# Pooled sums of q and k for the first two batches by accumulated TensorE products, with a new order of steps

## The chip, the cores and the metric

The kernel runs on one core of a Trainium2 chip. A core has a matrix engine (TensorE, PE in the profile), a vector engine (VectorE, DVE), an activation engine (ScalarE, ACT), a general engine (GpSimd, POOL) and a queue from which all transfers of this kernel start (SyncE, SP). Products land in PSUM, which has eight banks; all else lies in SBUF. Each engine works through its own queue in the order in which the program wrote it, and waits for the others by semaphores. The metric is device time in microseconds (us); lower is better.

## What is computed

The inputs are q, k and v of 8 batches, 8 heads, 576 tokens and 64 channels in float32, and the weights of a feed-forward layer, which arrive as float64 (512 x 1024 and 1024 x 512, with a scale vector). Cut to what matters:

```python
q_d = q.reshape(B, H, 144, 4, D).mean(axis=3)      # likewise k_d, v_d
out_up = np.repeat(sm_attn(q_d, k_d, v_d), 4, axis=2)
mask = np.abs(pos[:, None] - pos[None, :]) < 4
out_local = softmax(scale * q @ k.T where mask) @ v
x = (out_up + out_local) as [4608 tokens, 512]
h = x @ w_in
solu = h * softmax(h)
ln = (solu - mean) / np.sqrt(var + 1e-06) * g_ln
out = ln @ w_out
```

The attention has a pooled part, in which four neighbouring tokens are added up to one of 144 (the division by four is put into later scales), and a local part, in which a token sees three neighbours on each side.

## The kernel before

**Attention, batch by batch.** The 8 heads are taken as 4 pairs. For each pair, q and k are turned so that channels lie on partitions (`qT`, `kT`, 128 x 576: 64 channels of two heads), and then summed over four tokens (`qd`, `kd`, 128 x 144). `Batch.pair_steps` does that with VectorE transposes and two `sums` (line 419, a VectorE reduction). The first two batches are `EarlyBatch`: q and k are loaded so that a partition holds six neighbouring tokens (96 partitions, `TT` = 6), and `EarlyBatch.pair_steps` turns them with TensorE: for each of six token phases t and two heads, a product of the data with the unit matrix (line 557, tiles `qp` and `kp`), into a tile of two PSUM banks of which 288 numbers each are used. A copy (lines 263 on ScalarE or 265 on VectorE) brings them to `qT` and `kT` in token order, and the two `sums` follow as steps 5 and 6 of the pair.

`Pooled` makes the scores of 144 by 144 tokens (line 788, `sd`), the softmax (lines 795 to 812), turns it (line 823, `pdt`) and multiplies by the pooled v (line 844, `po`). `Local` and, from batch 3, `PairOfLocals` do the local part in windows of 64 tokens: scores (lines 607 and 695, `sc`), softmax, turning (line 655, `plt`), product with v (lines 665 and 753, `xp`).

**The feed-forward part** takes 36 tiles of 128 tokens. `xhl` splits x into two numbers `xh` and `xl` of reduced width (lines 1017 and 1020), `ffn_in` makes h with 24 products of 512 columns (line 862), and the softmax, the mean and the variance; `ffn_back` and `ffn_ut` turn the result by way of device memory and VectorE; `ffn_out` makes the output with 24 products (line 986). The weights are brought from float64 to pairs of reduced numbers in 16 pieces (`Weights.piece`, lines 364 to 412).

**Fillers.** `keep_clock` issues two products of no use (line 1043, tile `warm`); 24 such steps are in the plan.

**The order.** The functions above are generators. A plan lists all their steps in a natural order: 24 fillers first, then batch by batch the loads, pairs, attention, weights and feed-forward tiles. `ORDER` is a permutation of the plan's numbers, and the steps are run, that is written to the engines' queues, in that order; nothing is reordered afterwards. A step whose number is in `OTHER` uses a second engine for its work where the code offers one (`engine(usual, instead)`). Since the two early batches have 6 steps for each pair, the plan has 2029 steps.

```python
    for n in ORDER.split():
        now[0] = int(n)
        fn, args = plan[now[0]]
        fn(*args)
```

Of the kernel before, what the change touches and what calls it, by code (L numbers as in the profile page):

```python
# [137 lines left out]
def pooled_local_attention_then_solu_ffn(  # L138
# [10 lines left out]
    nc = tc.nc  # L149
# [884 lines left out]
    def row(steps, n):  # L1034
        for _ in range(n):
            step(next, steps)
# [119 lines left out]
```

## Time and profile before

| | |
|---|---|
| median of 3 runs | 589.33 us (589.28 to 589.5) |
| the profiled execution | 585.0 us |
| its span, first to last instruction | 583.2 us |
| mean granted TensorE clock | 0.999 |
| busy: PE, DVE, ACT, POOL | 564.1, 469.3, 333.8, 299.5 us |
| moved by DMA | 99.59 MB |

The profile is of one execution. A row of a group gives the line, the engine, the operation, the tile written and those read, the shapes, the count, the busy time in us and the mean of one instruction in ns, and behind the second bar the idle time of the engine ahead of it. A row of a timeline begins with the start in us from the span's start and the length. A row of waits names the engine and line that waited, the one that it waited for, and the us in total, the number of times and the longest. In the rows by stage, each engine has its busy us in the stage and its number of instructions. The ends of matmul records are modelled, so a step's length is read from its start to the start of the next one; a float32 product takes two records.

### The profile page before, as it was taken

The page shows a single profiled execution, that of the slowest core. Times are in us where ns is not written, and L with a number is a line of the kernel's source. Part 1 is how long each engine was busy: PE and PEld are TensorE (multiplying, and loading weights), DVE is VectorE, ACT ScalarE, POOL GpSimd, SP SyncE. Part 2 cuts the span into 40 slices and gives each one's busy share as a digit, 9 for nine tenths or more (in the row PEclk, how much of TensorE's full clock was granted, in tenths as well). Part 3 has the DMA queues.
Part 4 walks back from the last instruction along what each step waited for, and adds up shares of the span by engine and source line. Part 5 has one row for each costly group of instructions (what it writes and reads, how often), then busy time and mean ns, then how long its engine had stood idle before and what let it go on. Part 6 is the DMA issues. An engine that isn't in the chain of part 4 may idle for free.

```text
span 583.2 us, 15261 instructions
## 1 busy us (share of the span) xinstructions
PE 564.1 (97%) x5852; PEld 434.1 (74%) x5852; DVE 469.3 (80%) x779; ACT 333.8 (57%) x750; POOL 299.5 (51%) x447
## 2 busy tenths in 40 slices
PE   7899998999999999999999999999999999999996
PEld 3676666777787777877777777777787777788875
DVE  7989999898988879998977967899878877545541
ACT  4778678468546646565565753466445654444442
POOL 3657677957454745648533546356433752334120
PEclk9999999999999999999999999999999999999999
DMA  8997767787877888876867976766755145304230
GB/s 280 286 213 187 189 148 193 200 193 171 228 160 185 188 191 169 194 198 157 208 153 195 228 190 167 212 157 159 195 163 148 56 145 164 127 36 163 90 110 37
DMA packets 207113, 99.59 MB, mean 171 GB/s; under 512 B 163136, under 2 KB 193344, under 8 KB 207040
## 3 DMA queue, kind: packets, MB, share of 16 engines
q1 hardware_dynamic: 207040, 98.61, 66.3%
q8 instruction: 46, 0.75, 0.6%
q14 instruction: 27, 0.22, 0.1%
HBM read 65.54 MB, written 27.79 MB: 160 GB/s over the span
## 4 chain that ended last, share of the span: by engine, by line
PE 64%; DVE 14%; SPq 7%; DMA 5%; ACT 4%; issue 3%; POOL 2%; POOLq 0%; DVEq 0%
PE o L986 27%; PE h L862 25%; SPq L286 4%; DMA v<-u 3%; PE po L844 2%; PE sd L788 2%; PE xp L753 1%; PE pdt L823 1%; PE sc L607 1%; PE sc L695 1%; DVE w L375 1%; DVE qd_flat L419 1%; DVE nmx L870 1%; SPq L942 1%; DVE e L877 1%
## 5 line engine op out<-in xcount | busy, mean ns | idle before, releaser
L986 PE MATMUL o<-wo_h,uh 128*128 128x512 f32 x288 | 116.6, 405 | 1.5 <-ACT osb L993 0.8
L862 PE MATMUL h<-wi_h,xh 128*128 128x512 f32 x288 | 116.9, 406 | 0.8 <-DVE e L877 0.6
L862 PE MATMUL h<-wi_h,xl 128*128 128x512 f32 x288 | 114.1, 396 | 0.7 <-POOL xl L1020 0.7
L986 PE MATMUL o<-wo_l,uh 128*128 128x512 f32 x288 | 113.8, 395 | 0.0
L862 PE MATMUL h<-wi_l,xh 128*128 128x512 f32 x288 | 113.7, 395 | 0.0
L986 PE MATMUL o<-wo_h,ul 128*128 128x512 f32 x288 | 78.9, 395 | 0.0
L972 POOL TENSOR_TENSOR ul<-v,uh 128x512 fp32r<-128x512 f32 x40 | 51.9, 1297 | 42.8 <-ACT uh L969 41.6
L874 ACT ACTIVATE e<-h,nmx 128x1024 f32<-128x1024 f32 x36 | 40.2, 1116 | 49.1 <-DVE nmx L870 45.5
L986 PEld LDWEIGHTS o<-wo_h,uh 128*128 128x128 f32 x288 | 54.0, 188 | 16.8 <-ACT osb L993 1.5
L862 PEld LDWEIGHTS h<-wi_h,xh 128*128 128x128 f32 x288 | 54.1, 188 | 15.8 <-issue 2.9
L862 PEld LDWEIGHTS h<-wi_h,xl 128*128 128x128 f32 x288 | 54.1, 188 | 15.4 <-POOL xl L1020 2.1
L986 PEld LDWEIGHTS o<-wo_h,ul 128*128 128x128 f32 x288 | 54.0, 188 | 13.4 <-DVE ul L972 0.3
L870 DVE TENSOR_REDUCE nmx<-h 128x1 f32<-128x1024 f32 x36 | 43.8, 1216 | 24.2 <-PE h L862 24.2
L986 PEld LDWEIGHTS o<-wo_l,uh 128*128 128x128 f32 x288 | 54.1, 188 | 12.0
L862 PEld LDWEIGHTS h<-wi_l,xh 128*128 128x128 f32 x288 | 54.1, 188 | 11.9
L877 DVE SCALAR_TENSOR_TENSOR e<-h,e 128x1024 f32<-128x1024 f32 x36 | 43.8, 1217 | 14.2 <-ACT e L874 14.0
L969 ACT ACTIVATE uh<-v 128x512 fp32r<-128x512 f32 x70 | 42.9, 624 | 18.5 <-issue 7.1
L963 DVE STREAM_TRANSPOSE v<-v 128x512 f32<-128x512 f32 x70 | 46.4, 689 | 7.6 <-DMA v<-u 7.5
L993 ACT ACTIVATE osb<-o,s 128x512 f32<-128x512 f32 x36 | 24.6, 682 | 40.0 <-PE o L986 22.1
L1020 POOL TENSOR_TENSOR xl<-x,xh 128x512 fp32r<-128x512 f32 (+1 forms) x26 | 32.9, 1268 | 22.5 <-ACT xh L1017 22.2
L487 POOL TENSOR_TENSOR vs<-vs 72x512 f32<-72x512 f32 x24 | 31.9, 1328 | 17.5 <-DMA vs<-in_v_dram 9.0
L882 POOL TENSOR_SCALAR nmu<-su 128x1 f32<-128x1 f32 x36 | 8.1, 226 | 60.1 <-DVE e L877 57.2
(128 smaller groups left out, 1116.3 us busy)
## 6 DMA issues: line engine op xcount, KB each, us to landing
u<-e SPq DMA_DIRECT2D x35, 512.0 KB
v<-u SPq DMA_DIRECT2D x140, 128.0 KB
vs<-in_v_dram SPq DMA_DIRECT2D x32, 288.0 KB
out_dram<-osb SPq DMA_DIRECT2D x36, 256.0 KB
qm<-in_q_dram SPq DMA_DIRECT2D x96, 72.0 KB
km<-in_k_dram SPq DMA_DIRECT2D x96, 72.0 KB
vw<-in_v_dram SPq DMA_DIRECT2D x80, 64.0 KB
vw<-in_v_dram SPq DMA_DIRECT2D x40, 128.0 KB
```

What stands on the lines that cost most here:

```text
L286: nc.sync.dma_start(t[nm][Q * 32:Q * 32 + 32, pr], src[b, 2 * pr + par, :, dh * 32:dh * 32 + 32].rearrange("(k t) d -> t k d", t=32),)
L487: eng.tensor_tensor(out=vs[:, :, 0:2 * D], in0=vs[:, :, 0:2 * D], in1=vs[:, :, 2 * D:4 * D], op=ALU.add)
L862: nc.tensor.matmul(hps[:, n, :], src[:, cc, :], wt[:, cc, n * 512:(n + 1) * 512], start=(cc == 0 and src is xh and wt is wi_h), stop=(cc = ...
L870: nc.vector.tensor_reduce(out=nmx, in_=hf, op=ALU.max, axis=AX.X, negate=True)
L874: nc.scalar.activation(e, hf, AF.Exp, bias=nmx, scale=1.0, accum_out=se)
L877: nc.vector.scalar_tensor_tensor(out=e, in0=hf, scalar=1.0, in1=e, op0=ALU.mult, op1=ALU.mult, accum_out=su)
L963: nc.vector.transpose(vg, vg)
L969: nc.scalar.activation(uh, tp, AF.Copy)
L972: (usual if v is None else engine(usual, nc.vector)).tensor_tensor(out=ul, in0=tp, in1=uh.bitcast(F32), op=ALU.subtract)
L986: nc.tensor.matmul(o, src[:, j, :], wt[:, 4 * g + j, :], start=(g == 0 and j == 0 and src is uh and wt is wo_h), stop=(g == 1 and j == 3 a ...
L993: nc.scalar.activation(osb, o, AF.Copy, scale=s)
L1020: engine(nc.gpsimd, nc.vector).tensor_tensor(out=l, in0=src, in1=h.bitcast(F32), op=ALU.subtract)
```

## The change

For the batches below `POOLED_ON_PE` = 2, `pair_steps` adds, behind the twelve products that turn q or k, fourteen more in the same PSUM tile: the 144 numbers behind the 288 of its first bank. Token 6p + t belongs to the pooled token (6p + t) // 4, so with p = 2m + e the pooled token is 3m + (6e + t) // 4: for each phase t, the products take the columns of the unit matrix for e = 0 and 1 and add into columns j of every m, accumulating over t. For t = 2 the two columns don't lie at a step that one output can have, and two products of 48 columns are made. The copy step then also copies the 144 sums to `qd` or `kd` on the same engine, the two `sums` steps fall away, and the plan has 2013 steps. `ORDER` and `OTHER` are new as a whole. In the new order the first loads of q and k are issued ahead of the first weight piece, and three filler steps stand ahead of the first turning, where seven stood before.

```diff
 ORDER = """
-7 192 160 6 193 194 24 195 196 197 161 162 25 163 164 8 165 198 199 166 168 167 169 170 176 12
-171 172 177 33 22 1 3 32 26 178 15 27 28 29 30 31 41 20 173 179 174 34 180 35 181 36 37 40 64
...
+18 21 24 25 184 8 26 30 27 20 185 186 187 31 28 29 152 188 189 32 33 190 34 56 153 154 155 156
+191 35 3 66 160 161 67 37 68 157 158 159 36 38 39 43 162 163 164 165 40 166 167 57 42 192 193
...
 """
@@
     FIRST_ON_PE = ()
+    POOLED_ON_PE = 2
@@ class EarlyBatch
+        by_pe = property(lambda self: self.b < POOLED_ON_PE)
@@ EarlyBatch.pair_steps
                             ident[0:self.TP, 0:self.TP], start=True, stop=True,
                         )
+                if self.by_pe:
+                    three = tp[:, 0, n:n + SD].rearrange("x (m j) -> x m j", j=3)
+                    turn = ident[0:self.TP, 0:self.TP].rearrange("p (m e) -> p m e", e=2)
+                    for at_t, (t, js, es) in enumerate((
+                        (0, (0, 2, 1), (0, 2)), (1, (0, 2, 1), (0, 2)),
+                        (2, (2, 3, 1), (1, 2)), (2, (0, 1, 1), (0, 1)), (3, (0, 3, 2), (0, 2)),
+                        (4, (1, 3, 1), (0, 2)), (5, (1, 3, 1), (0, 2)),
+                    )):
+                        for par in range(2):
+                            nc.tensor.matmul(
+                                three[rows(par), :, js[0]:js[1]:js[2]],
+                                self.qk[nm, pr][:, par, t],
+                                turn[:, :, es[0]:es[1]], start=at_t == 0, stop=at_t == 6,
+                            )
                 yield
                 copy(
                     engine(nc.scalar, nc.vector),
                     dst.rearrange("x (p a t) -> x p a t", a=2, t=HT),
                     tp[:, :, 0:n].rearrange("x a (t p) -> x p a t", t=HT),
                 )
-                yield
+                if self.by_pe:
+                    copy(
+                        engine(nc.scalar, nc.vector),
+                        self.qd[pr] if nm == "q" else self.kd[:, pr], tp[:, 0, n:n + SD],
+                    )
+                yield
+            if self.by_pe:
+                return
             sums(self.qd[pr], self.qT[:, pr])
             yield
             sums(self.kd[:, pr], self.kT[:, pr])
@@ prepare
-            row(bt.pair_steps(pr), 6 if bt.b < EARLY else 4)
+            row(bt.pair_steps(pr), 6 if POOLED_ON_PE <= bt.b < EARLY else 4)
```

201 rows, old and new, of tables (ORDER, OTHER) are left out of this document.

## The prediction

> **What bounds the kernel now.** I read the page's first two parts, then the busy time by stage, then TensorE's own timeline and waits, and last the groups. First the page: totals, then TensorE (PE) and VectorE (DVE) in 40 slices.
>
> ```profile
> PE 564.1 (97%) x5852; PEld 434.1 (74%) x5852; DVE 469.3 (80%) x779; ACT 333.8 (57%) x750; POOL 299.5 (51%) x447
> ...
> PE   7899998999999999999999999999999999999996
> ...
> DVE  7989999898988879998977967899878877545541
> ```
>
> PE is busy throughout; DVE is as full only in the first fifth. What a change early in the kernel is worth is therefore read from that fifth, and what it leaves behind must still pass through PE. I cut the span where PE changes its work: the first turned q (9.75), the first product of the feed-forward part (57.30), the first product of token tile 4 (118.60), and the last product's end.
>
> ```profile
> core 0: us, PE busy (x) PEld busy (x) DVE busy (x) ACT busy (x) POOL busy (x), PEclk, DMA share, GB/s
> 0.00:9.75 9.75, 6.09 (x15) 1.58 (x15) 6.67 (x18) 3.25 (x4) 1.59 (x10) 1.00 0.80 277
> 9.75:57.30 47.55, 42.74 (x884) 31.61 (x883) 43.83 (x84) 37.40 (x101) 31.74 (x28) 1.00 0.94 231
> 57.30:118.60 61.30, 58.68 (x817) 43.69 (x813) 58.64 (x101) 42.64 (x86) 48.21 (x56) 1.00 0.75 186
> 118.60:579.40 460.80, 456.54 (x4146) 357.25 (x4144) 360.13 (x581) 249.79 (x561) 218.00 (x356) 1.00 0.63 161
> ```
>
> Behind 118.6 us PE idles 4.26 us in 460.8: there the length of the run is the sum of PE's work. Ahead of it PE idles 4.81 and 2.62 us (7.4 together), and DVE idles 3.7 and 2.7: the two engines are nearly level. What PE waits for between 9.75 and 118.6:
>
> ```profile
> PE xp L665 <- ACT plT L263: 1.7, 1, 1.7
> PE sc L607 <- issue: 1.1, 1, 1.1
> PE sd L788 <- issue: 1.1, 1, 1.1
> PE h L862 <- POOL xl L1020: 0.7, 2, 0.4
> PE sd L788 <- ACT kT L263: 0.6, 1, 0.6
> PE qp L557 <- DMA qm<-in_q_dram: 0.3, 1, 0.3
> PE sd L788 <- ACT pdT L263: 0.3, 1, 0.3
> PE po L844 <- POOL vd L490: 0.2, 1, 0.2
> PE qp L557 <- ACT qT L263: 0.2, 1, 0.2
> PE sc L600 <- DVE x L578: 0.2, 1, 0.2
> ```
>
> The sums that the change removes do not stand here: no wait in this list names L419. Now PE's timeline (start, length, line, tile, count), for the pace of its steps.
>
> ```profile
> 3.32 6.49 PE L1043 MATMUL warm<-ident_b 128*128 128x512 bf16 x14 [3.32 <-DVE ident_b L216]
> 9.75 1.21 PE L557 MATMUL qp<-ident,qm 96*64 96x96 f32 x24
> 10.89 0.60 PE L1043 MATMUL warm<-ident_b 128*128 128x512 bf16 x2
> 11.43 1.21 PE L557 MATMUL kp<-ident,km 96*64 96x96 f32 x24
> ...
> 21.08 0.71 PE L788 MATMUL sd<-kd,qd_flat 64*64 64x144 f32 x12
> 21.71 1.21 PE L557 MATMUL qp<-ident,qm 96*64 96x96 f32 x24
> ...
> 36.10 1.21 PE L557 MATMUL kp<-ident,km 96*64 96x96 f32 x24
> 37.24 0.66 PE L655 MATMUL plt<-ident,pl 128*128 128x128 f32 x4
> 37.83 1.21 PE L557 MATMUL qp<-ident,qm 96*64 96x96 f32 x24
> 38.87 1.16 PE L557 MATMUL kp<-ident,km 96*64 96x96 f32 x24
> ```
>
> Turning one pair's q or k takes 24 records, two for each of 12 products, and from its start to the next step's start 1.04 us where the next step was ready (37.83 to 38.87) and 1.14 us where not (36.10 to 37.24). That tenth is a loss which the busy row hides. A filler pair costs 0.54 us (10.89 to 11.43); the first 14 records took 6.43.
>
> **The change, part by part.** *Products added.* Each of 16 groups (2 batches, 4 pairs, q and k) gets, for two heads, five products of 96 columns and two of 48: 14 products, 28 records, 20 x 96 + 8 x 48 = 2304 columns. The turning in front of them has 24 x 96 = 2304 too. Paced by columns, as qp, that is 1.04 us; paced by records it is 28/24 of that, 1.21. Downwards, the nearest row is sd: 12 x 144 = 1728 columns in 0.63 us (21.08 to 21.71), where parts of the array overlap, so 2304 columns in 0.84. Upwards, the outputs lie at steps of three in the bank, which no row of before shows; I bound that by every record taking twice its time, 2.1 us. I take 1.10, between the two readings of qp, whose operands, 96 rows and 64 columns of weights, these are: 16 x 1.10 = **+17.6 us of PE** (ends 13.4 and 33).
>
> The nearest rows for split outputs are these two scores, L607 written in one run of 64 and L695 in two of 32:
>
> ```profile
> L607 PE MATMUL sc<-kT,qT 64*64 64x64 f32 x640 | 14.3, 224 | 1.4 <-issue 1.1
> L695 PE MATMUL sc<-kT,qT 64*64 64x64 f32 x640 | 12.2, 221 | 0.0
> ```
>
> They cost the same, so I leave the price at 1.10. The Trainium skill (PSUM — Partial Sum Buffer, Specifications) says that lines there are 8 bytes, two of these numbers, and that "any non-contiguous AP slows matmuls significantly"; steps of three are not runs of 32, so by it the price goes towards the upper end, and the sum with it by up to 15 us. These rows neither bear it out nor deny it.
>
> *Sums removed, copies added.* The removed line (shortest, median, longest ns) and who waited for it, then the groups of ACT and DVE from which the rest is priced:
>
> ```profile
> L419 DVE TENSOR_REDUCE qd_flat<-qT x32: 701/740/753, 13.3 to 456.1; 128x144 f32<-128x576 f32 x32
> L419 DVE TENSOR_REDUCE kd<-kT x32: 696/742/756, 13.9 to 421.7; 128x144 f32<-128x576 f32 x32
> ...
>   PEld sd L788: 0.6, 2
> ```
>
> ```profile
> L263 ACT ACTIVATE kT<-kp 128x576 f32<-128x576 f32 x8 | 5.1, 642 | 1.6 <-PE kp L557 1.6
> L265 DVE COPY pdT<-pdt 72x288 f32<-72x288 f32 x15 | 6.6, 443 | 3.8 <-ACT pdT L263 3.6 <-PE pdt L823 0.3
> L265 DVE COPY qT<-qp 128x576 f32<-128x576 f32 x1 | 0.7, 749 | 0.0
> L803 ACT ACTIVATE pd<-sd,mxd 128x144 f32<-128x144 f32 x96 | 35.4, 378 | 1.5 <-DVE rsd L810 0.4
> L1020 DVE TENSOR_TENSOR xl<-x,xh 128x512 fp32r<-128x512 f32 x10 | 6.7, 676 | 2.4 <-ACT xh L1017 2.4
> L645 DVE TENSOR_TENSOR pl<-pl,rsl 128x512 f32<-128x512 f32 x4 | 2.7, 686 | 0.1
> ```
>
> DVE loses 16 x 0.74 = 11.8 us. By the new lists four of the sixteen turning copies go to DVE (one before) with their sums' copies: 3 x 0.75 and 4 x at most 0.44, 4.0 us. ACT gets twelve small copies (128x144 out of PSUM, as L803, 0.38 us: 4.5) less three of 0.64. The new list of steps done elsewhere gives DVE, ahead of tile 4, three subtractions of L1020 (2.0) and three products of L645 (2.1) that it did not have, and more small ones both ways. So of 11.8 us some 4 are left. ACT, 70 to 79% busy in these stages, hides its 2.6; DVE's relief is worth what PE waited for, not its own sum, and for the sums themselves only the weight load of two score steps waited, 0.6 us.
>
> *Numbering the steps.* Reading both lists against the plan, PE has the same work queued ahead of tile 4's first product, to within one score step of pooled attention more and one filler less (0.1 us), plus the added products; all sixteen groups lie ahead of it, and ahead of the first feed-forward product too. Behind it the same work remains. So the run is longer by what that point is late, unless the later stage's 4.26 us of idling changes; both orders change between feed-forward and other work about as often there (84 and 82 times), and I put it at nothing.
>
> *The start.* Loads of q and k go ahead of the first weight piece in SP's queue, and three filler pairs instead of seven stand ahead of the first turning. Four pairs then run later at 0.54. The 6.43 us of seven pairs are 3.8 us of work and 2.65 of slow pace, and the slow pace meets whatever stands there: 0, between -2.65 and +2.65. From the view of the loads in the first 70 us:
>
> ```profile
> qm<-in_q_dram SPq DMA_DIRECT2D x8, 288.0 KB
> ```
>
> Two such loads at the 277 GB/s of the first stage put the first weight piece back by 2.1 us; the turning covers it on PE, and the sums that left DVE cover it there. If that cover is gone, 2.1 us.
>
> *Waits added.* The bank of a turned q or k is held for a second group and a second copy, 1.1 + 0.38 us longer; the next turning on the same two banks waits behind it, and with it all of PE's queue, which is in order. The longest such wait now is 0.2 us (qp for qT). The rows of q and k in SBUF are read 1.1 us longer per group, so batch 1's first load, which takes that room, holds SP's queue, and the weights behind it, by as much. I leave both inside the range.
>
> **The sum.** +17.6 products, +0.1 other steps. Taken back: the waits for ACT, POOL and DVE in the list above, 3.9 us, since PE is now later than its suppliers; the two "issue" stalls (2.2) name no supplier and stay. Of the hidden tenths, 106 PE steps lie between 9.75 and tile 4: 10.6 us if each had one; I take 3.5, a third. 17.7 - 3.9 - 3.5 = **+10.3 us**. The profiled execution is 585.0 us with a span of 583.2; the median of the runs is 589.33, and I add the difference to that: 599.6.
>
> **Rivals.** *Faster: PE has more room than its busy row says.* If DVE's level queue is what makes PE's steps start one by one, its relief brings back all 7.4 us of idling and all 10.6 us of tenths, and products that overlap as sd's do cost 13.4: 13.5 - 18.0 = -4.5, 584.8 us. It decides below (18.0 / 16) 1.12 us a group with everything taken back. For it: DVE at 58.64 of 61.30. Against it: qp has the shape of the new products and doesn't overlap, and PE's waits do not name the sums. The Trainium skill (Perfetto Trace Analysis, Identifying the Most-Contended Engine) would judge PE by its weight loads, 74% of the span here, not by 97%. By that rule a quarter of PE is free; the stage behind 118.6 us, where PE hardly ever stands still, speaks against it.
>
> *No change.* The products at 1.10 are swallowed by the 18.0 us: 17.7 - 18.0, 589.
>
> *Split outputs at half pace.* 33 in place of 17.6 us, and the same 7.4 back: +25.7, 615. For it: no row shows such outputs. Against it: L695. It is the case that the Trainium skill's page (PSUM — Partial Sum Buffer, Specifications) describes.
>
> *A replanned order that fits worse*, with nothing taken back: +17.7, 607.
>
> **How the numbers follow.** Slower by about 10 as summed (from 591 to 605): 0.58. Nothing taken back: 0.10. Half pace, wholly or in part (605 to 615): 0.12. No change: 0.07; 0.2%, 1.2 us, is about what a measurement of this kernel can tell. Faster: 0.13. That makes 0.13 / 0.07 / 0.80. The range runs from the edge of no change, 588.2, to 611, which leaves out the faster case and the last of half pace. The likeliest case alone has 591 to 605.
>
> **What would show it.** Records of L557-like products: 28 more a group and 0.84 to 1.21 us each from start to start; above 1.3, half pace is at work. The first feed-forward product some 8 to 12 us later than 57.3, and tile 4's by about 10 later than 118.6, with the distance from there to the end unchanged: if that distance moves by over 3 us, the order of the late steps did what I put at nothing. PE idling under 4 us between the first turning and tile 4. L419 at 24 + 24. The forecast is wrong if the new groups overlap, or if PE's steps close up by more than a third of the tenths.

## The result, and the profile after

The changed kernel takes 606.70 us in the median (603.71 to 609.98), the kernel before on the same chip 589.31. The quotient of the two medians is 1.0295; the ratio of the single runs, which is used from here on, is 1.0344, with a 95% interval of 1.0299 to 1.039. The kernel is slower, as forecast, and 7 us slower than the 599.6 us forecast: inside the stated range (588.2 to 611), outside the likeliest case (591 to 605). Executions of one kernel differ by more than the 1.2 us that the prediction took for what a measurement can tell: over all series those of the kernel before lie between 582.2 and 592.8 us. The profiled execution took 603.71 us with a span of 601.8, which is 18.6 more than before.

From the page of the changed kernel, the same rows as before, and the granted clock under them:

```profile
PE 580.1 (96%) x6300; PEld 452.4 (75%) x6300; DVE 473.9 (79%) x776; ACT 327.3 (54%) x746; POOL 304.4 (51%) x454
...
PE   7997999799999999999999999998999999999996
...
DVE  4798999989998977986988888999587864754642
...
PEclk9998999999999999999999999999999999999999
```

PE has 448 records (16 x 28) and 16.0 us of busy time more. What is new otherwise stands in the first slices: DVE begins at 4 where it had 7, PE has two more slices of 7, and the clock has one of 8.

The busy time by stage, cut at the same events as before (first turned q, first feed-forward product, first product of tile 4, end of the last product), columns as before:

```profile
0.00:6.42 6.42, 2.98 (x6) 0.64 (x6) 2.34 (x9) 1.28 (x1) 1.58 (x10) 1.00 0.70 212
6.42:70.05 63.63, 58.56 (x1297) 48.53 (x1297) 51.11 (x93) 39.86 (x112) 30.14 (x23) 0.97 0.84 218
70.05:135.22 65.17, 62.05 (x866) 46.55 (x865) 62.40 (x107) 43.23 (x94) 39.19 (x43) 0.97 0.79 180
135.22:597.95 462.73, 456.55 (x4137) 356.65 (x4135) 358.01 (x570) 242.24 (x540) 233.53 (x378) 1.00 0.60 156
```

Tile 4's product comes at 135.22 instead of 118.60, 16.6 us later; the last stage is 1.9 us longer. PE idles 5.07 and 3.12 us in the two stages between, 8.2 where it was 7.4, and the clock of both is 0.97 where it was 1.00.

PE's waits between the first turning and tile 4, and behind tile 4, each from the top:

```profile
PE sc L630 <- DVE x L265: 3.1, 1, 3.1
PE pdt L846 <- DVE qd_flat L265: 2.3, 1, 2.3
PE qp L559 <- ACT kd L263: 1.0, 1, 1.0
```

```profile
PE sd L811 <- DVE pdT L265: 2.3, 2, 2.0
```

None of the waits that the prediction took back stands at the top now; other ones, mostly for DVE, have come in their place. PE's timeline shows the new products (L573) and what follows the waits of 2.3 and 3.1 us:

```profile
10.57 1.23 PE L573 MATMUL kp<-ident,km 96*64 96x96 f32 x28
11.63 1.16 PE L559 MATMUL qp<-ident,qm 96*64 96x96 f32 x24
12.62 1.23 PE L573 MATMUL qp<-ident,qm 96*64 96x96 f32 x28
13.68 1.16 PE L559 MATMUL kp<-ident,km 96*64 96x96 f32 x24
...
51.20 0.53 PE L846 MATMUL pdt<-ident,pd 64*72 64x64 f32 x12 [2.26 <-DVE qd_flat L265]
51.66 1.11 PE L678 MATMUL plt<-ident,pl 128*128 128x128 f32 x4
52.57 1.06 PE L1066 MATMUL warm<-ident_b 128*128 128x512 bf16 x2
...
70.05 0.58 PE L885 MATMUL h<-wi_h,xh 128*128 128x512 f32 x1
...
118.16 0.94 PE L630 MATMUL sc<-kT,qT 64*64 64x64 f32 x40 [3.11 <-DVE x L265]
```

A group of 28 records takes 1.06 us to the next step's start (10.57 to 11.63, 12.62 to 13.68), the turning in between 0.99 (11.63 to 12.62). Behind the pause of 2.26 us the filler pair takes 0.99 (52.57 to 53.56), where it takes 0.54 elsewhere. The granted clock says why, in windows of 4 us at this place and at the next long pause (3.11 us ahead of 118.16):

```profile
52.00:56.00 4.00, 4.00 (x46) 2.93 (x46) 2.68 (x6) 1.78 (x5) 1.84 (x2) 0.62 1.09 285
120.00:124.00 4.00, 4.00 (x35) 3.22 (x32) 4.00 (x8) 1.81 (x5) 2.40 (x4) 0.59 0.82 207
```

In both, PE is busy all the time at about 0.6 of its pace; in windows of 1 us within them, the clock reads 0.50 from 52 to 55 and from 120 to 123. Summed over windows of 1 us, (1 - clock) x length comes to 1.70 us at each place, which is 3.4 us at half pace. The Trainium skill (TensorE: Matmul & The Clock Gate, Part 1) has PE run at half rate after an idle window of 3.4 us; the length and the pace agree, while pauses of 2.26 and 3.11 us were enough here.

What DVE did in the first 20 us, after and then before, as windows, and DVE's first pieces of work after:

```profile
0.00:20.00 20.00, 15.63 (x270) 11.53 (x272) 8.96 (x22) 5.66 (x11) 2.86 (x11) 1.00 0.81 251
```

```profile
0.00:20.00 20.00, 15.20 (x180) 8.54 (x184) 16.04 (x33) 10.84 (x23) 7.47 (x14) 1.00 0.93 291
```

```profile
9.11 0.76 DVE L265 COPY qT<-qp 128x576 f32<-128x576 f32 x1 [5.74 <-PE qp L573]
...
13.89 0.76 DVE L265 COPY qT<-qp 128x576 f32<-128x576 f32 x1 [1.56 <-PE qp L573]
...
18.92 0.61 DVE L818 TENSOR_REDUCE mxd<-sd 128x3 f32<-128x432 f32 x1 [2.53 <-PE sd L811]
```

The new lists give DVE the copy of the first turned q; it stands first in DVE's queue, and the weight steps behind it wait with it until 9.11. DVE has done 7 us less by 20 us than before, ACT and POOL some 5 less each.

Up to tile 4, DVE is busy for longer than before and not for less time: 115.8 us against 109.2, although the sums have gone (15.3 us of L419 have become 4.4). About as much other work has come to DVE, and two steps of the weights take 6.6 us longer for the same number on the same shapes. Their groups up to tile 4, after and then before, and last what stands in DVE's queue ahead of the copy for which PE waits 3.1 us:

```profile
L379 DVE SCALAR_TENSOR_TENSOR w<-w,w 128x512 int32<-128x512 int32 x12 | 13.1, 1096 | 0.2
L375 DVE SCALAR_TENSOR_TENSOR w<-w,w 128x512 int32<-128x512 int32 x12 | 10.3, 862 | 0.2
```

```profile
L379 DVE SCALAR_TENSOR_TENSOR w<-w,w 128x512 int32<-128x512 int32 x12 | 8.6, 719 | 0.2
L375 DVE SCALAR_TENSOR_TENSOR w<-w,w 128x512 int32<-128x512 int32 x12 | 8.2, 681 | 0.2
```

```profile
112.70 1.66 DVE L375 SCALAR_TENSOR_TENSOR w<-w,w 128x512 int32<-128x512 int32 x1
114.39 3.18 DVE L379 SCALAR_TENSOR_TENSOR w<-w,w 128x512 int32<-128x512 int32 x1
117.50 0.61 DVE L265 COPY x<-xp 128x448 f32<-128x448 f32 x1
```

Such a step mostly takes 0.69 us. The longest, here and between 40 and 49 us, lie beside products of POOL that follow one another without a gap (here from 112.33 to 117.03); that POOL is the cause is likely and not shown.

Three numbers per kernel carry the experiments below: when tile 0's and tile 4's first products and the last output half-step start; how long PE was idle up to there; and what it lost to slow pace, (1 - granted clock) summed over windows of 1 us (2 us in the last stage). All are us, and of one execution each. The slow pace at the very start is not counted, since the clock's row reads 1.00 there.

| kernel | tile 0: at; idle; slow | from there to tile 4: at; idle; slow | from there to the end: at; idle; slow |
|---|---|---|---|
| before | 57.3; 8.5; 0 | 118.6; 2.6; 0 | 569.7; 3.4; 0 |
| after | 70.1; 8.5; 1.7 | 135.2; 3.1; 1.7 | 588.2; 5.3; 0 |
| e1 | 83.8; 23.8; 22.2 | 150.1; 3.2; 3.4 | 603.0; 5.3; 0 |
| e2 | 77.4; 9.7; 3.4 | 138.7; 2.5; 0 | 591.5; 4.8; 0 |
| e3 | 70.0; 13.4; 8.5 | 137.5; 3.1; 5.1 | 592.1; 5.3; 1.7 |
| e4 | 83.5; 6.0; 0 | 148.5; 3.1; 1.7 | 603.1; 5.3; 1.7 |
| g1 | 57.2; 8.3; 0 | 119.4; 3.3; 0 | 571.1; 4.1; 0 |
| g2 | 68.5; 15.8; 10.2 | 134.8; 3.1; 3.4 | 587.7; 5.3; 0 |
| f1 | 69.3; 6.9; 1.7 | 135.4; 3.2; 1.7 | 590.4; 5.4; 1.7 |

With them the 18.6 us come apart: products 16 x 1.06 = 17.0; idle time and slow pace up to tile 4 (8.5 + 3.1 + 3.4) - (8.5 + 2.6) = +3.9; idle time behind it +2.0; and -4.3 is left over, which no row names.

### The profile page after: what moved, and what is told of

Its sections match the earlier page's. It is cut to its first block, busy times and chain, and to the rows that moved or that the text cites. A ratio compares the mean times of both kernels' runs of the same rounds, so it can differ in the third digit from the quotient of the medians.

```text
span 601.8 us, 16123 instructions
## 1 busy us (share of the span) xinstructions
PE 580.1 (96%) x6300; PEld 452.4 (75%) x6300; DVE 473.9 (79%) x776; ACT 327.3 (54%) x746; POOL 304.4 (51%) x454
## 4 chain that ended last, share of the span: by engine, by line
PE 84%; DVE 7%; issue 2%; DMA 2%; SPq 2%; POOL 1%; ACT 1%; DVEq 0%; ACTq 0%; POOLq 0%
PE h L885 31%; PE o L1009 30%; PE po L867 3%; PE sd L811 3%; PE pdt L846 2%; PE xp L776 2%; PE sc L630 2%; PE sc L718 2%; PE warm L1066 2%; PE plt L678 1%; PE xp L688 1%; DMA vw<-in_v_dram 1%; SPq L305 1%; PE qp L559 1%; PE kp L559 1%
## 5 line engine op out<-in xcount | busy, mean ns | idle before, releaser
L995 POOL TENSOR_TENSOR ul<-v,uh 128x512 fp32r<-128x512 f32 x43 | 56.5, 1318 | 37.4 <-ACT uh L992 34.8
L1009 PEld LDWEIGHTS o<-wo_h,ul 128*128 128x128 f32 x288 | 53.9, 188 | 13.5 <-DVE ul L995 0.4
L1009 PEld LDWEIGHTS o<-wo_l,uh 128*128 128x128 f32 x288 | 54.4, 189 | 11.8
L1043 POOL TENSOR_TENSOR xl<-x,xh 128x512 fp32r<-128x512 f32 (+1 forms) x22 | 26.8, 1222 | 27.3 <-ACT xh L1040 25.8
L487 POOL TENSOR_TENSOR vs<-vs 72x512 f32<-72x512 f32 x27 | 36.5, 1353 | 4.7 <-issue 4.4
```

The costliest lines, as they stand in the source:

```text
L487: eng.tensor_tensor(out=vs[:, :, 0:2 * D], in0=vs[:, :, 0:2 * D], in1=vs[:, :, 2 * D:4 * D], op=ALU.add)
L995: (usual if v is None else engine(usual, nc.vector)).tensor_tensor(out=ul, in0=tp, in1=uh.bitcast(F32), op=ALU.subtract)
L1009: nc.tensor.matmul(o, src[:, j, :], wt[:, 4 * g + j, :], start=(g == 0 and j == 0 and src is uh and wt is wo_h), stop=(g == 1 and j == 3 a ...
L1043: engine(nc.gpsimd, nc.vector).tensor_tensor(out=l, in0=src, in1=h.bitcast(F32), op=ALU.subtract)
```

## The experiments

Ratios are to the kernel before on the same chip, with 95% intervals. Names: *order* is the new `ORDER` and `OTHER`, *products* the sums on PE, *slow pace* what the granted clock takes. In the expectations, broadly, A is the theory that PE's queue sets the early stage, B that the new order fits worse, C that pauses of PE bring on half pace, D that DVE sets the stage. The numbers of a kernel's lines differ by a few from those of after.

**e1: the new order, the sums by VectorE.** The products go, and the copy step sums with line 419's operation instead.

```diff
-                if self.by_pe:
-                    three = ...
...
                 if self.by_pe:
-                    copy(
-                        engine(nc.scalar, nc.vector),
-                        self.qd[pr] if nm == "q" else self.kd[:, pr], tp[:, 0, n:n + SD],
-                    )
+                    sums(self.qd[pr] if nm == "q" else self.kd[:, pr], dst)
```

> The new order is kept, the added products are left out, and each of the sixteen sums is a VectorE reduction again, in the step that copies qT or kT. Theory A (the products are paid for on PE's queue, one us for each us): PE loses 16 x 1.06 = 17.0 us, and the changed kernel's time falls by about that, less what 16 reductions of 0.74 us on VectorE cost in new waits: 589 to 595 us. Theory B (the new order fits worse, with or without the products): it stays at 600 or more. Theory C (pauses of PE in the new order throw its clock to half pace): 600 or more too, with a granted clock under 0.995 and pauses of over 2 us on PE.

617.55 us, 1.0537 [1.0496, 1.0578]: slower than after, although PE has 17 us less to do. Its windows from 20 us on:

```profile
20.00:40.00 20.00, 16.82 (x302) 12.25 (x300) 16.15 (x29) 10.73 (x34) 6.07 (x6) 0.69 0.66 182
40.00:60.00 20.00, 11.79 (x145) 8.81 (x138) 18.32 (x30) 10.24 (x24) 10.27 (x9) 0.73 0.91 239
60.00:80.00 20.00, 14.92 (x223) 11.78 (x221) 16.16 (x28) 10.29 (x30) 6.90 (x7) 0.67 0.57 124
```

PE stands still 16 of 60 us and runs the rest at 0.7 of its pace. Without the products, and with the sums on DVE, this order starves PE.

**e2: the old order, the products.** The old `ORDER` and `OTHER`; products and copies as in after, and steps 5 and 6 of an early pair do nothing.

```diff
+            if self.by_pe:
+                yield
+                yield
+                return
             sums(self.qd[pr], self.qT[:, pr])
```

> The old order and the old list of other engines are kept; the sums of the first two batches come from the added products, and the two steps that held the reductions are empty. Theory A: +17.0 us on PE less what of the old idling (7.4 us before tile 4) is taken back: 599 to 607 us, as the changed kernel. Theory B: the products alone cost little in the order made without them, under 595 us, and the rest of the 17 to 20 us is the new order's. Theory C: between them, by how many pauses of PE over 2 us there are.

606.39 us, 1.0353 [1.0302, 1.0404], as slow as after. So the products alone, without the new order, cost all of it. In its profile DVE has time to spare (100.2 us busy up to tile 4) and waits for PE and for ACT, here in a window and in DVE's waits up to tile 0:

```profile
40.00:60.00 20.00, 17.05 (x313) 15.01 (x311) 8.11 (x19) 8.91 (x24) 3.88 (x5) 0.83 0.59 140
```

```profile
DVE mxd L821 <- PE sd L814: 11.8, 5, 5.7
DVE pdT L266 <- ACT pdT L264: 10.2, 1, 10.2
```

**e3: four of fourteen products**; PE has 12 us less to do, all else is as in after.

```diff
-                        (0, (0, 2, 1), (0, 2)), (1, (0, 2, 1), (0, 2)),
...
-                        (4, (1, 3, 1), (0, 2)), (5, (1, 3, 1), (0, 2)),
+                        (0, (0, 2, 1), (0, 2)), (2, (2, 3, 1), (1, 2)),
```

> The changed kernel with 4 of the 14 added products in each group (8 records of 28: 6 x 96... in all 4 x 96 + 4 x 48 = 576 of 2304 columns); the rest of each sum is left out. Copies and order are those of the changed kernel. Theory A: 16 x 0.75 = 12 us less PE work, so about 12 us less than the changed kernel, 592 to 596 us. Theory B: less than 4 us off, over 601. Theory C: over 600, as long as the pauses of PE at 49 and 115 us stay, since they are not made by the products.

604.71 us, 1.0305 [1.0216, 1.0395]: not distinguishable from after. In the profiled execution (607.53 us) tile 0 starts at 70.0, where it did with all products: the 12 us have become idle time (+4.9) and slow pace (+6.8). The window in which most of the slow pace lies:

```profile
40.00:60.00 20.00, 13.57 (x170) 11.69 (x166) 17.05 (x28) 11.21 (x28) 11.10 (x10) 0.63 0.79 185
```

**e4: the products issued twice**, the second round over the first; 17 us more for PE.

```diff
-                    for at_t, (t, js, es) in enumerate((
+                    for at_t, (t, js, es) in 2 * list(enumerate((
...
-                    )):
+                    ))):
```

> The changed kernel with every added group of products issued twice into the same place, the second over the first. Theory A: another 16 x 1.06 = 17.0 us, 620 to 626 us. Theory B: the slope is smaller, under 615 us, since a part of the second set fills pauses that the order leaves. Theory C: more PE work fills pauses, so the granted clock rises towards 1.0 and the time rises by less than 13 us.

619.52 us, 1.0575 [1.053, 1.0619]: 13 us over after (619.52 - 606.70, of two series; by the ratios 2.3%, 13.5 us). Upwards PE's work is paid for: tile 0 comes 13.4 us later, and the rest comes out of idle time (8.5 to 6.0) and slow pace (1.7 to 0). In after, then, the early stage seems to stand near the point at which PE's work and the rest are level: less of it gains nothing that can be told (e3), more costs most of its price.

**r5 and r7: the start.** r5 gives the four copy steps that the new lists had put on DVE back to ACT; r7 also moves the first weight piece's load and its first five steps ahead.

```diff
-    other = {int(n) for n in OTHER.split()}
+    other = {int(n) for n in OTHER.split()} - {27, 33, 383, 385}
```

```diff
-18 21 24 25 184 8 26 30 27 20 185 186 187 31 28 29 152 188 189 32 33 190 34 56 153 154 155 156
+18 21 184 24 25 8 185 186 187 188 189 26 30 27 20 31 28 29 152 32 33 190 34 56 153 154 155 156
```

> The changed kernel with the four turning copies and sums' copies that its list gives to VectorE (plan numbers 27, 33, 383 and 385) left on ScalarE. Theory A (PE's queue alone sets the early stage): no change, 602 to 610 us, the first feed-forward product at 70 us. Theory D (in the new order VectorE sets it, and it starts late: the first of these copies stands ahead of the first weight conversion in VectorE's queue and waits 5.7 us for PE): VectorE starts on the weights at about 6 us instead of 10, and the first feed-forward product and the end come 2 to 5 us earlier. Theory C (pauses and half pace): the pause of 2.3 us at 49 us, which waited for one of these copies, is gone with its 1.7 us of slow pace, 2 to 4 us in all.

> As the kernel with the four copies on ScalarE, and the first weight piece is loaded ahead of q and k, with its first five conversion steps ahead of the first turning. Theory D: VectorE is busy from 5 us on, as before the change, and the first feed-forward product comes another 1 to 4 us earlier. Theory A: no gain, or a loss of up to 2 us, since the first turning waits for its load. The whole kernel stays behind the one before under both, by 8 us or more.

609.2 us, 1.0423 [1.0364, 1.0482], and 608.82 us, 1.0419 [1.0371, 1.0468]. Neither gains, and tile 0 comes at 73.7 and 72.1. DVE does no more in the first 20 us (7.3 and 7.4 us busy, after 9.0); from r7's DVE waits up to 72 us:

```profile
DVE w L366 <- ACT w L364: 11.3, 3, 8.0
```

The copies now stand in ACT's queue, ahead of ACT's own part of the weights, and DVE waits for that: the head of the queue that blocks has only changed engines. So giving that copy back cures nothing. The pause of 2.3 us at pdt stays in r5, under the name "issue".

**r8: before with 17 of 24 fillers left out** (those that stand behind the first turning).

```diff
     def keep_clock(n):
+        if n not in (7, 6, 8, 12, 22, 1, 3):
+            return
```

> The kernel before with only the seven filler steps that stand ahead of the first turning; the 17 later ones issue nothing. Theory A: PE loses 17 x 0.5 = 8.5 us of work and the time falls by 4 to 8 us, to 580 to 585. Theory C: what the fillers filled becomes pauses, PE drops to half pace in 3.4 us pieces (1.7 us each), and the time does not fall, 588 to 596. Theory D: VectorE sets the stage, so without half pace the time stays within 2 us.

589.09 us, 1.0057 [1.0025, 1.0089]. 17 x 0.54 = 9.2 us less for PE, and the kernel is not faster but slower by about 0.6%: up to tile 0 idle time goes from 8.5 to 10.9 and slow pace from 0 to 5.1. The fillers are not room into which products can be put free of charge.

**r9: the old order, products for three pairs only**, paid for with six fillers; as e2, with

```diff
+            by_pe = self.b == 0 and pr < 3
...
+        if n in (15, 20, 0, 18, 14, 10):
+            return
```

> The old order; only three pairs of batch 0 have their sums on PE (6 groups, 6.4 us of PE and 6 x 0.74 = 4.4 us less on VectorE), and the six fillers that stand among these steps (3.2 us) issue nothing. Theory A: +3 us, 592. Theory D: up to 4 us faster than before, 585 to 588, as VectorE is the fuller engine of that stage. Theory C: the same as D if no pause of over 2 us arises, 590 to 594 if one does.

593.46 us, 1.0117 [1.0032, 1.0203]. A small dose gains nothing either. How much it costs stays unclear, for its executions spread from 588.58 to 599.02. Six groups less six fillers are 6 x 1.06 - 6 x 0.54 = 3.1 us; 0.0117 x 585.3 (before's median there) is 6.8, and the interval goes from 1.9 to 11.9.

**g1 and g2: the sums for nothing.** The question was whether the new order is good or bad by itself. The small copy takes 144 of the turned numbers, and no engine sums anything; all that waits for qd and kd stays. g1 has the old order, g2 the new one. The diff is g2's against after, from which the products go too, as in e1; g1 adds the same small copy to before, as in e2, and empties steps 5 and 6.

```diff
                     copy(
                         engine(nc.scalar, nc.vector),
-                        self.qd[pr] if nm == "q" else self.kd[:, pr], tp[:, 0, n:n + SD],
+                        self.qd[pr] if nm == "q" else self.kd[:, pr], tp[:, 0, 0:SD],
                     )
```

> The old order with the sums of the first two batches left out: neither the sixteen reductions on VectorE nor products; a copy of 144 turned numbers stands for each sum. It gives the most that the change could have won in the old order, with its products free. Theory A (PE's queue sets the early stage): VectorE's relief is worth the waits of PE that name an engine, 3.9 us, so 581 to 585 beside 585 of before. Theory D (VectorE sets it): up to 8 us off, 577 to 581. Theory C: nothing or worse, 585 to 590, if PE now pauses and drops to half pace.

> The same in the new order: the changed kernel without its products, with a copy of 144 turned numbers for each sum. Theory B (the order fits worse by itself): still 10 us or more behind before, 597 to 605. Theory A: 17.0 us less than the changed kernel, 588 to 592. Theory C: as B, with a granted clock of 0.98 or less and more idling on PE than the changed kernel's 8.5 us ahead of the first feed-forward product; idling and slow pace together grow by about the 17 us of products that are gone.

g1 590.82 us, 1.0042 [1.0, 1.0084]; g2 605.66, 1.0331 [1.025, 1.0411]. These two with the four kernels above make a table of ratios:

| | sums on VectorE | sums for nothing | products on PE |
|---|---|---|---|
| old order | 1 (before) | 1.0042 (g1) | 1.0353 (e2) |
| new order | 1.0537 (e1) | 1.0331 (g2) | 1.0344 (after) |

In the old order, taking the sums off VectorE is worth nothing that can be told, and the products cost 3.1% over g1, 18 us, which is 1.14 a group. In the new order the same products cost 0.1% over g2, well within the intervals: it is 3% slow with them and without. Where g2's time goes, in a window and at the top of PE's waits up to tile 0:

```profile
40.00:60.00 20.00, 13.75 (x143) 11.24 (x144) 17.24 (x30) 11.47 (x28) 10.66 (x9) 0.60 0.79 185
```

```profile
PE qp L559 <- ACT kd L263: 5.1, 1, 5.1
```

The 17.0 us of products taken out of after have come back as +7.3 of idle time and +8.5 of slow pace ahead of tile 0 (15.8 of 17.0), and tile 0 starts 1.5 us earlier in the profiled execution.

**f1: after with a lighter DVE.** Two of the conversion steps (lines 370 and 375) are left out for all 16 weight pieces.

```diff
             yield
-            nc.vector.tensor_scalar(out=ti, in0=ti, scalar1=3, ...)
             yield
-            nc.vector.scalar_tensor_tensor(out=ti, in0=hi, scalar=-0x40000000, ...)
             yield
```

> The changed kernel, products and all, with two of VectorE's four conversion instructions left out for every weight piece (lines 370 and 375, 0.57 and 0.69 us; the weights are then meaningless numbers): 16 x 1.26 = 20 us less on VectorE, some 11 of them ahead of the first feed-forward product. Theory D: that product comes 4 us or more earlier than 70 us and the end with it, 598 to 603 us. Theory A: within 2 us of the changed kernel. Theory C: earlier by the pauses that it takes away and their slow pace, 3 to 6 us.

600.87 us, 1.0261 [1.0198, 1.0323], some 5 us less than after by the ratios; the intervals overlap a little, so it is likely and not certain. The profiled execution is the slowest (605.82) and shows none of the gain: tile 0 starts at 69.3 against 70.1, tile 4 at 135.4 against 135.2. DVE, 94.5 us busy up to tile 4 where after has 115.8, waits for PE:

```profile
DVE mxd L811 <- PE sd L804: 9.7, 4, 5.1
DVE qT L265 <- PE qp L566: 9.3, 2, 6.5
```

So DVE's load is at most a small part of it. The wait of 3.1 us for DVE's copy is gone with the long weight steps, but PE idles as much in that stage (3.2 us), now with 2.2 us of it under "issue"; and with DVE relieved, PE's queue holds tile 0 at the same place.

**h1: e2 without the 17 fillers** (r8's edit).

```diff
+        if n not in (7, 6, 8, 12, 22, 1, 3):
+            return
```

> The old order with the products, and only the seven filler steps ahead of the first turning: the 17 later ones, 8.5 us of PE, issue nothing. With products in their place PE is the fuller engine, so theory A has 6 to 9 us less than the 606 of the old order with products: 597 to 601. Theory C: the fillers' time comes back as idling and slow pace, 603 to 608. Theory D: within 3 us of 606.

602.38 us, 1.0279 [1.0212, 1.0347], against e2's 1.0353 [1.0302, 1.0404]: perhaps 4 us better; the intervals overlap, so it stays unclear. No kernel of all these is faster than before.

## Why the prediction was right, and where not

Right was the sign, and the main term: in the old order the products cost their whole time on PE's queue (e2 against g1). The size of +10.3 was not right, since one term of the sum had the wrong sign. Of the prediction's cases the one nearest to the result is *a replanned order that fits worse*, at 607, not the one taken as likeliest, and e1 and g2 bear its condition out: the order alone is slower too. That its sum, with no wait added, meets the result is in part luck.

- **Products added.** 1.10 was taken, 1.06 was measured: 17.0 us against 17.6. Of the two readings of qp, that by columns (1.04) is nearer. In the old order, where nothing else changes, the time that they cost is 1.14 a group by the ratios (g1 to e2). PE had no room: the rule of the Trainium skill by its weight loads (Perfetto Trace Analysis, Identifying the Most-Contended Engine), 74% here, would have left a quarter of PE free, and e2 and e4 speak against that.
- **Split outputs at half pace.** Not so: 28 records with outputs at steps of three took 1.06, 24 with whole ones 0.99. The Trainium skill's rule (PSUM — Partial Sum Buffer, Specifications) that such outputs slow products significantly did not show, and the measurement decides.
- **Sums removed.** That DVE's relief is worth only what PE waited for is borne out in the old order, where DVE is 8.3 us less busy up to tile 4 (g1, 100.8) and the run no faster: 1.0042. The rival *PE has more room* and that of *no change* fall with it and with e2. Of 11.8 us the prediction left DVE "some 4" of relief; in after it has 6.7 us more to do, for the new order moves work to it and its weight steps take longer.
- **Waits taken back, -3.9: the step that failed.** Those waits did mostly go, and the reason given, "PE is now later than its suppliers", holds in the old order, where DVE waits for PE (e2). But in the new order the suppliers moved too, and waits of 3.1, 2.3 and 1.0 us came in their place, each of the two long ones with 1.7 us of slow pace behind it, which the prediction had nowhere but at the start. In place of -3.9 the runs have +3.9. The prediction had named the kind of two of these under *Waits added* and left it inside the range: `pdt` and `qp` read nothing of the small copies (`qd_flat`, `kd`) that they wait for, they take room in the pair of PSUM tiles (`ps_a`) that those copies empty. The 2.3 and 1.0 us stand where it had seen 0.2, and g2's 5.1 is of that kind too.
- **Hidden tenths, -3.5.** What is left over in the account is -4.3, all of it ahead of tile 4, and the size fits by luck. The same account up to tile 4 leaves -5.2 for g2, which has no products, -1.4 for e2 and +0.3 for g1: most of it is the new order's, and not PE's steps closing up because PE is late.
- **The start**, put at nothing. Its slow pace is 2.0 us in after: six filler records take 3.10 (3.32 to 6.42) where three pairs at 0.54 make 1.62, the first turning 1.41 for 0.99, its products 1.16 for 1.06. Before it was 2.65. The cover that was named for the later weight piece, the sums that left DVE, was not there: DVE's queue begins with a copy that waits for PE. What that is worth could not be separated, as r5 and r7 only moved the wait.
- **The later stage**, put at nothing: +2.0, below the 3 us named. It is the order's: `sd` waits 2.3 us for DVE's pdT there in after, and PE's idle time in that stage is 5.3 to 5.4 in all kernels of the new order in the table and 3.4 to 4.8 in those of the old.
- **The marks.** Tile 0 came 12.8 us later (8 to 12 were named), tile 4 16.6 (10), and PE idled 8.2 us between the first turning and tile 4 (under 4). All three say that little or nothing was taken back. L419 stands at 24 + 24:

```profile
L419 DVE TENSOR_REDUCE kd<-kT 128x144 f32<-128x576 f32 x24 | 17.7, 740 | 0.4
L419 DVE TENSOR_REDUCE qd_flat<-qT 128x144 f32<-128x576 f32 x24 | 17.4, 730 | 0.0
```

What the prediction did not think of is that order and products don't add up: each alone costs 3% or more (e2 for the products, g2 or e1 for the order), and both together 3.4%. The new order leaves holes in PE's early work, which with the slow pace behind them are about as large as the products (g2: 7.3 and 8.5 us); the products fill them. One reading fits e3, e4, g2 and f1: two things hold tile 0 near 70 us in the new order, PE's queue with the products and the suppliers' queues without them, so that taking away either (e3 and g2, or f1) shows the other. That is argued, not shown: no kernel relieves both. Which of the suppliers holds the new order, DVE, ACT behind it, or the loads, also stays open; the wait that leads differs from kernel to kernel (DVE in after, ACT's kd in g2, DVE's kd in e1). What the new order does to DVE can be named: in the eight traces with it DVE's weight step L379 (L372 in f1, L380 in some) takes 0.80 to 1.10 us in the mean, in those with the old order 0.72 to 0.73; its share of the time was not measured by itself.

## What to carry to other kernels

Count on work that moves onto the engine that is busy throughout at its full price, however small its instructions, unless a run with that work left out altogether shows that its old place was on the path; that run (g1) is cheap, and here it would have answered before anything was moved. Try new work and a new order each by itself and together, for their costs don't add: beside e2 the products cost everything and the order nothing, beside g2 the order everything and the products nothing. And a saving on an engine that loses its pace when it pauses is to be counted in granted clock as well as in idle time.

## What the runs showed of the hardware

- PE's slow pace comes in pieces of 1.70 us lost, 3.4 us at half pace; in after it stands behind pauses of 2.26 and 3.11 us, while before's longest pause behind the start, 1.7 us, has none behind it. So less work can take as long: 12 us less in e3 became 4.9 idle and 6.8 slow, 17.0 less in g2 7.3 and 8.5, and before without 17 fillers is no faster (1.0057).
- Products whose outputs lie at steps of three float32 in PSUM, accumulated over seven, run at nearly the pace of ones with whole rows: 2304 columns in 1.06 us (28 records) against 0.99 (24).
- The same DVE instruction on the same shape (L379, 128x512) takes 0.69 us in most places and 1.40 to 3.18 in others, where POOL is at work beside it. With POOL at work a few also take 0.69 (61.85 us), and then POOL's product is the long one (L490, 1.91 us at 61.20, for 0.73 at 35.53).
